# Feature-map attention and a maxout feed-forward on one core: numerators from 64-row matmul pairs, with the row maxima applied as a factor on GpSimd

## The chip, the cores and the metric

The kernel runs on one core of a Trainium2 chip. The metric is the device time of one execution in microseconds. Below, PE is TensorE, DVE is VectorE, ACT is ScalarE, POOL is GpSimd and SP is the engine that issues most DMAs.

## The reference

Attention without a softmax: q and k of each of 8 x 8 heads (576 tokens, 64 channels) are projected to 128 features and turned to two exponentials, and the output feeds a maxout layer. With the shapes cut to what matters:

```python
def phi(x):                                   # x: (8, 8, 576, 64)
    proj = np.einsum('bhsd,df->bhsf', x, w_phi)              # df = 128
    proj = proj - np.max(np.abs(proj), axis=-1, keepdims=True)
    return np.concatenate([np.exp(proj), np.exp(-proj)], axis=-1)
q_p, k_p = phi(q), phi(k)
kv = np.einsum('bhsf,bhsd->bhfd', k_p, v)
z = np.sum(k_p, axis=2)
num = np.einsum('bhsf,bhfd->bhsd', q_p, kv)
den = np.einsum('bhsf,bhf->bhs', q_p, z)[..., None] + 1e-06
x = num / den                                 # then to (4608, 512)
h = maximum(maximum(x @ w1, x @ w2), x @ w3)  # 4608 x 768
out = h @ w_out                               # 4608 x 512, float32
```

With m the largest absolute projection of a row, the two halves are exp(p - m) and exp(-p + m): m doesn't cancel between them, but a common factor of both halves does (but for the 1e-06).

## The kernel before

Attention goes by 16 **units** of four heads, two units to a batch; the feed-forward goes by nine **chunks** of 512 tokens, one to a batch and a last one (chunk 8) of the 64 tokens that each batch has over. The steps of a unit, with the names used below:

- **loads**: q, k and v come as 128 x 1152 tiles (18 tiles of tokens by 64 channels). From unit 4 on q and k come in float32 through SP's queue (line 474) and POOL casts them into `qk_bf` (480); units 1 to 3 use a converting DMA that POOL issues (463). In `qk_bf` of units from 4 on, the columns of a token tile hold 64 channels of q, then 64 of k.
- **T**: a transposing DMA (512) gives `qkT`, q's channels on partitions 0 to 63, k's on 64 to 127.
- **G**: projections in 64-row matmuls, one of q and one of k at a time (535), into `psq` and `psk`. ACT makes the exponentials `Ek` of k (548); DVE reduces the maxima of q into `mqp`, those of k into `mk` (554).
- **R, V**: PE transposes the maxima of q into `pmT` (562), `mT` is a copy of it (566), and a DMA writes it as one row into `qkT` (570), at partition 64, where a channel of k stood.
- **M**: `psm`, the features by tokens of q: one matmul of 512 columns for each four token tiles (614), whose weights `wphi_m` hold w_phi in 64 rows and -1 in the 65th, so that p - m comes out of the product, though the matmul takes all 128 rows. ACT makes the two `Eq` of it (627), with scales 1 and -1.
- **vab**: POOL multiplies v with a factor `em` from the maxima of k, one instruction for each sign (589).
- **K**: `kvps`, keys times values in 64-row matmuls (643), and their copy `kv_sb` (648).
- **N and x**: numerators and denominators `psn`, 20 matmuls of 65 columns in two steps for each pair of heads (661), and the division on DVE (667, 668).
- **X**: a transposing DMA (691) of `x_sb` into `xT`, by which the chunk of the unit's batch becomes ready.

A chunk multiplies xT with w2 - w1 and w3 - w1 (`ups`, 714; the differences are made once at the start, 784), takes the larger of both and zero on ACT (722) and DVE (724, 720), and makes the down product `ops`: from these maxima with w_out (746), and straight from xT with w1 times w_out (741), which is multiplied once at the start (812). It is copied out at 754 and stored at 761.

What sets the order: `manual_schedule()` leaves it to the program. `PLAN` is a table with one word for each step, number, engine, buffer slots and a start; `plan()` hands the steps their engine and slots from it and issues the code in the table's order. Every engine works its own queue in order. The eight PSUM banks are one pool of slots, `bank`, for all tiles in PSUM. `fill()` puts idle products (`idler`) into gaps of PE's table.

Of the kernel before, what the change touches and what calls it, by code (L numbers as in the profile page):

```python
# [12 lines left out]
ALU = mybir.AluOpType  # L13
# [37 lines left out]
QK = 3  # L51
OSB = 4
GATES = (None, (0, 0), (1, 0), (2, 0))
# [43 lines left out]
0G@0.70 2D0@0.70 4A@0.70 10S0@0.70 3D@0.90 6S0@1.18 1G@1.25 8S@1.66 86G0@1.75 13S@2.14 85G@2.60 15S0@2.62 1076G@3.45 12A1@3.98  # L97
158G2@4.25 7D@4.96 159G@5.10 5D@5.46 16T1@5.61 9A@5.94 1079G@5.95 17D0@6.30 22T002300@7.08 27T45@7.30 26D@7.55 30D@8.15 14A@8.43
25D@8.76 23A@9.05 20T6@9.20 18T7@9.31 31D@9.37 21D@9.97 227G1@10.01 28A@10.12 19D@10.20 42T14@10.35 29A@10.62 45D@10.81
32T26@10.96 24A@11.11 46D@11.15 37T75@11.26 35D@11.49 34A@11.60 89T1@11.60 91T3@12.04 47A0@12.09 40D@12.10 44A@12.34 48G0@12.48  # L100
39A@12.68 90D1@12.71 61T20@12.86 33A@13.16 64T7@13.31 92D@13.33 228G@13.60 38A@13.65 36D@13.95 95T111311@14.10 66A@14.14
49G@14.45 41D@14.56 65A@14.63 43A@15.12 99D@15.16 110T67@15.27 63A@15.46 50G@15.57 55T5@15.61 98D@15.77 1077G@15.85 111A@15.94
1090T4@16.06 113D@16.38 62A@16.43 1088T1@16.66 56A@16.91 114D@16.98 67T2@17.26 97A@17.40 1086T6@17.49 1089D0@17.59 51A@17.89
69A@18.14 87D1@18.21 53G@18.29 58T0@18.34 1087D@18.34 88S@18.46 68A@18.48 57A@18.82 164T1@18.89 361S1@18.94 1091D@18.96
59A@19.30 93T2@19.34 52G@19.41 162T6@19.45 165D2@19.59 112A@19.79 166T5@19.90 163D@20.21 60A@20.28 105T41@20.36 54G@20.52
1078G@20.80 106A@20.83 108D@20.83 70T070@20.95 96A@21.32 160D2@21.44 167D@21.54 161S@21.69 94D@21.76 109D@21.98 100T64@22.05
296S0@22.17 115T53@22.27 101A@22.52 72D@22.59 362S1@22.65 1094T2@22.75 119D@22.96 102A@23.02 117A@23.50 104D@23.66 116A@23.84
1096T0@24.05 107A@24.18 103D@24.26 124A1@24.68 118D@24.87 120A@24.93 127G1@25.07 71A@25.18 1095D@25.21 183T003400@25.44
1097A@25.59 173T16@25.66 168T57@25.88 123A@26.09 177D@26.13 1098T2@26.23 185A@26.24 170A@26.73 186D@26.74 125G@27.00 175A@27.22
176D@27.35 137T01@27.52 184A@27.71 171D@27.95 77T30@27.98 126G@28.12 138A@28.23 1092T1@28.29 78D0@28.56 139A@28.71 172D@29.18  # L110
1099A@29.20 122G@29.23 79T5@29.58 174A@29.70 187D@29.79 75T3@29.90 1093A@30.18 140T0@30.21 121G@30.35 229D3@30.39 131T2@30.44
76D1@30.50 141A@30.69 73T6@30.89 142A@31.03 80D0@31.11 128T4@31.21 132A@31.37 11G@31.47 364G0@31.62 74D1@31.73 178T13@31.76
133A@31.85 143T105@31.98 130A@32.34 181D@32.35 129A@32.82 182D@32.96 188T26@33.08 233T1@33.31 145A@33.33 192D@33.57 144A@33.73
134T4@33.88 191D@33.91 196A0@34.13 234D0@34.25 146T51@34.34 190A@34.38 198G0@34.53 148T0@34.65 135A@34.72 147D0@34.90
235T2@35.06 231T1@35.17 189A@35.20 149D1@35.52 199A@35.55 136A@35.70 152T5@35.74 193T6@36.05 232D@36.14 179A@36.18 81T0@36.29
83T4@36.60 197G@36.62 169A@36.67 153D0@36.76 150T1@36.91 194A0@37.16 154T7@37.31 236D@37.38 180A@37.41 195S@37.56 151D1@37.60
242T115611@37.72 84A@37.90 247T23@38.05 155D@38.22 297S0@38.34 156T1@38.39 82D@38.69 230S@38.82 215T047@38.87 157A@38.95
1080D@39.16 426S1@39.30 249A@39.60 1081D@39.78 1104T0@40.09 244A@40.09 1082D@40.40 248A@40.58 1106T1@40.95 250D@41.02 216A@41.07
365G@41.37 251D@41.63 1102T4@41.81 1107A1@42.06 246D@42.23 1105A@42.56 366S1@42.64 1110T2@42.67 245D@42.84 243A@43.06
1084D@43.45 1108T3@43.54 1103A@43.55 1111A@44.05 1085D@44.07 252T10@44.50 217A@44.55 1083D@44.69 257T56@44.72 237T42@44.83  # L120
1109A@44.95 1112T7@45.17 240D@45.31 259A@45.45 299G2@45.66 239A@45.79 255D@45.91 1124T3@46.04 254A@46.28 1113D@46.52 253A@46.77
# [119 lines left out]
1421S@265.97 1431A@266.06 1444T4@267.11 1416D2@267.36 1411T@267.97 1417S@268.12 1445D@268.22 1443D@268.84 1454T0@269.26  # L241
1412D0@269.51 1459T@270.12 1413S@270.28 1455T@271.41 1460D1@271.66 1461S@272.43 1462T2@272.70 1456A3@272.95 1463T@273.56
1457S@273.71 1474T7@274.85 1475T@275.07 1464D2@275.10 1466T1@275.39 1476A0@275.64 1467T@275.82 1465S@275.87 1477A@275.89
1470T4@276.47 1471T@276.68 1468A1@276.72 1469A@277.09 1472D3@277.25 1473S@277.68
"""


# [627 lines left out]
```

## Time and profile before

| | us |
|---|---|
| median of 3 runs | 285.63 |
| lowest and highest run | 283.97, 286.08 |
| span of the profiled execution | 282.5 |
| its own time around the span | not given; median less span is 3.1 |
| POOL casts of q and k (line 480), 24 | 27.5 |
| POOL products with v (line 589), 36 | 68.2 |
| DVE reductions (line 554), 160 | 97.3 |
| ACT exponentials of k and of q (548, 627), 320 | 160.0 |

In the profile a row of a group names the line, the engine, the operation, what it writes and reads, how often, its busy time and the mean duration in ns, and behind the second bar how long the engine stood idle just ahead of such instructions and what ended that. Durations of matmuls overlap, since they are pipelined: the distance from one start to the next is what one costs. Rows of the timeline begin with start and duration. PEld is the load of weights into PE, and SPq and POOLq are the engines' DMA queues.

### The profile page before, as it was taken

How to read it: one execution, taken by the hardware profiler on the slowest of the kernel's cores; microseconds unless marked ns; L12 is line 12 of the kernel's file. 1: busy time of each engine (PE TensorE's matmuls, PEld its weight loads, DVE VectorE, ACT ScalarE, POOL GpSimd, SP SyncE). 2: the span in 40 equal slices, each digit the busy share in tenths (PEclk: the TensorE clock that was granted, in tenths of full speed). 3: DMA queues.
4: the chain of work that ended last, by engine and by line, in shares of the span. 5: the costliest groups of instructions: out<-in, count | busy, mean ns of one | idle time of the engine just before them, and what ended most of it. 6: DMA issues, size and time to landing. Idle time of an engine off the chain costs nothing.

```text
span 282.5 us, 8556 instructions
## 1 busy us (share of the span) xinstructions
PE 271.2 (96%) x3521; PEld 154.0 (54%) x3560; DVE 211.6 (75%) x443; ACT 192.3 (68%) x449; POOL 113.2 (40%) x106
## 2 busy tenths in 40 slices
PE   8888979999999999999999999999999999999995
PEld 3565764566555644764556456555455465444443
DVE  4998989998877888679989876997477594254141
ACT  2897979898889779998585879977707961311111
POOL 8373567748176418913760563053033600000000
PEclk9999999999999999999999999999999999999999
DMA  7999999888999999999797866954975105600154
GB/s 202 240 206 282 280 273 240 266 204 167 300 363 198 175 308 300 194 165 277 212 199 129 246 235 124 166 102 167 186 177 116 40 4 104 137 2 0 37 123 139
DMA packets 68337, 51.45 MB, mean 182 GB/s; under 512 B 48778, under 2 KB 53066, under 8 KB 68298
## 3 DMA queue, kind: packets, MB, share of 16 engines
q1 hardware_dynamic: 63876, 45.74, 66.8%
q0 software_dynamic: 4000, 4.92, 10.0%
q8 instruction: 28, 0.46, 0.7%
q10 hardware_dynamic: 422, 0.24, 0.3%
q14 instruction: 11, 0.09, 0.1%
HBM read 34.64 MB, written 9.44 MB: 156 GB/s over the span
## 4 chain that ended last, share of the span: by engine, by line
PE 80%; DMA 11%; DVE 4%; issue 2%; SPq 1%; DVEq 0%
PE ups L714 31%; PE ops L746 14%; PE ops L741 10%; DMA wout_bf<-in_moe_w_out_dram 6%; PE psn L661 6%; PE kvps L643 5%; PE psm L614 5%; PE psq L535 4%; PE pm L812 2%; DMA out_dram<-osb 2%; DMA xT<-x_sb 2%; DVE x_sb L668 2%; DMA k_raw<-in_k_dram 1%; DVE mqp L554 1%; DVE mk L554 1%
## 5 line engine op out<-in xcount | busy, mean ns | idle before, releaser
L714 PE MATMUL ups<-xT,w_bf 128*128 128x512 bf16 x416 | 100.3, 379 | 1.4 <-DMA xT<-x_sb 0.3
L589 POOL TENSOR_TENSOR vab<-v_raw,em 128x1152 bf16<-128x1152 f32 (+1 forms) x36 | 68.2, 1907 | 67.2 <-ACT em L585 50.9
L548 ACT ACTIVATE Ek<-psk 128x512 bf16<-128x512 f32 (+1 forms) x160 | 80.8, 569 | 13.9 <-PE psk L535 10.1
L627 ACT ACTIVATE Eq<-psm 128x512 bf16<-128x512 f32 (+1 forms) x160 | 79.2, 570 | 7.3 <-PE psm L614 7.0
L714 PEld LDWEIGHTS <-w_bf 128*128 128x128 bf16 x432 | 41.0, 98 | 47.4 <-issue 0.4
L554 DVE TENSOR_REDUCE mqp<-psq 128x4 bf16<-128x512 f32 (+1 forms) x80 | 48.8, 631 | 6.3 <-PE psk L535 4.4
L746 PE MATMUL ops<-wout_bf,hT 128*128 128x512 bf16 (+2 forms) x215 | 49.3, 367 | 1.0 <-issue 0.5
L554 DVE TENSOR_REDUCE mk<-psk 128x4 f32<-128x512 f32 (+1 forms) x80 | 48.5, 628 | 2.4 <-PE psk L535 1.7
L720 DVE TENSOR_TENSOR hT<-hT,ups 128x512 bf16<-128x512 bf16 x54 | 36.1, 682 | 16.4 <-PE ups L714 12.7
L668 DVE TENSOR_TENSOR x_sb<-psn,rden 128x320 bf16<-128x320 f32 x64 | 31.5, 492 | 2.2
L746 PEld LDWEIGHTS <-hT 128*128 128x128 bf16 x228 | 21.1, 98 | 21.7
L722 ACT ACTIVATE hT<-ups 128x512 bf16<-128x512 f32 x33 | 19.1, 603 | 17.3 <-PE ups L714 15.8
L661 PEld LDWEIGHTS <-Eq 128*128 128x128 bf16 x640 | 25.0, 97 | 7.8 <-ACT Eq L627 0.2
L754 DVE COPY osb<-ops 128x512 f32<-128x512 f32 (+1 forms) x22 | 14.7, 669 | 16.8 <-PE ops L746 16.0
L661 PE MATMUL psn<-kv_sb,Eq 128*128 128x65 bf16 x640 | 26.9, 194 | 0.2 <-DVE mqp L554 0.2
L754 ACT COPY osb<-ops 128x512 f32<-128x512 f32 (+2 forms) x16 | 8.9, 562 | 23.2 <-PE ops L746 22.6
L741 PE MATMUL ops<-xT 128*128 128x512 bf16 x90 | 24.1, 380 | 0.3
L535 PE MATMUL psq<-w,qkT 64*128 64x128 bf16 x288 | 24.3, 217 | 0.1
L535 PE MATMUL psk<-w,qkT 64*128 64x128 bf16 x288 | 24.0, 217 | 0.4 <-ACT Eq L627 0.4
L535 PEld LDWEIGHTS <-qkT 64*128 64x128 bf16 x576 | 16.5, 94 | 12.0 <-issue 8.9
L614 PE MATMUL psm<-qkT,wphi_m 128*128 128x512 bf16 (+1 forms) x70 | 22.1, 358 | 0.0
L480 POOL CAST qk_bf<-q_raw 128x1152 bf16<-128x1152 f32 x12 | 13.8, 1147 | 20.3 <-DMA out_dram<-osb 9.4
(73 smaller groups left out, 230.9 us busy)
## 6 DMA issues: line engine op xcount, KB each, us to landing
v_raw<-in_v_dram SPq DMA_DIRECT2D x16, 576.0 KB
out_dram<-osb SPq DMA_DIRECT2D x64, 128.0 KB
q_raw<-in_q_dram SPq DMA_DIRECT2D x12, 576.0 KB
k_raw<-in_k_dram SPq DMA_DIRECT2D x12, 576.0 KB
w_bf<-in_moe_w_dram POOLq DMA_DIRECT2D x3, 768.0 KB, 20.3
qk_bf<-in_k_dram POOLq DMA_DIRECT2D x3, 288.0 KB, 13.9
qk_bf<-in_q_dram POOLq DMA_DIRECT2D x3, 288.0 KB, 13.4
wout_bf<-in_moe_w_out_dram POOLq DMA_DIRECT2D x1, 768.0 KB, 17.7
```

Of the source, the lines that this page charges most:

```text
L535: nc.tensor.matmul(ps()[:, i, :], lhsT=cols[r, :], rhs=w2[r, c, :], start=True, stop=True)
L548: nc.scalar.activation(Ek[s]()[:, tiles_of(t0, n), :], of(1), EXP, scale=1.0 - 2.0 * s)
L554: nc.vector.tensor_reduce((mq, mk)[c]()[:, tiles_of(t0, n)], of(c), AXX, ALU.max, apply_absolute_value=True)
L589: (nc.vector if n_.eng == "DVE" else nc.gpsimd).tensor_tensor(vab()[:, g, t0:t1, 0:D], vb()[:, t0:t1, :], em()[:, g, t0:t1].unsqueeze(2).t ...
L614: nc.tensor.matmul(psm()[:, 0:w], lhsT=wphi_m, rhs=rhs, start=True, stop=True)
L627: nc.scalar.activation(Eqb()[s][:, cols], psm()[:, 0:w], EXP, scale=1.0 - 2.0 * s)
L661: nc.tensor.matmul(psn()[:, c, :], lhsT=Eqb()[g][:, t0:t0 + P], rhs=kv()[:, pr, ab, g, :], start=(g == 0), stop=(g == 1))
L668: nc.vector.tensor_tensor(x_sb()[:, pr, :, ab, :], psn()[:, :, 0:D], rden().to_broadcast([P, 5, D]), ALU.mult)
L714: nc.tensor.matmul(ups(), lhsT=w_bf[i + 1][:, ct, j * P:(j + 1) * P], rhs=tokens_of(ct), start=(ct == 0), stop=(ct == CT - 1))
L720: nc.vector.tensor_tensor(hT()[:, j, :], hT()[:, j, :], ups(), ALU.max)
L741: nc.tensor.matmul(ops_()[:, 0:width], lhsT=tile_of(ct, tt), rhs=line_w[c_i > MOVE][:, ct, cols], start=(ct == 0), stop=False)
L746: nc.tensor.matmul(ops_()[:, 0:width], lhsT=hT()[:, j, tt * P:(tt + 1) * P], rhs=wout_bf[:, j, cols], start=False, stop=(j == JT - 1))
```

## The change

Units 0 to 3 stay as they are. From unit 4 on (`FROM`), a second function `attention_b` stands in for `attention`:

- q and k come by converting loads that POOL issues, into a `qk_bf` that holds all of q and then all of k; it has four slots instead of three. The float32 tiles of v, and of unit 0's q and k, share one pool of four slots (`RAW`).
- After T, partitions 0 to 63 hold one token tile and 64 to 127 the next, so that 64-row pairs are two token tiles of the same tensor. G does the tiles of q first, then those of k; the last tile of both is done as a full matmul of 256 columns against `w2`, which holds zeros beside w_phi.
- M no longer uses the row of maxima: two 64-row matmuls of 512 columns, for two banks of `psm`, go side by side. M needs only T, no longer R and V.
- The exponentials of q have constant offsets instead (`SHIFTS`): exp(p - 79) and exp(-p + 9). `Eq` has three slots instead of two.
- The maxima become a factor: `mT` is exp(-2m + 88), a DMA writes it to a row in memory (`row`), another broadcasts that row to 128 partitions (`fac`, one slot), and POOL multiplies the first half of `Eq` with it, in three instructions, two of 1024 elements and one of 256 for each partition. Numerators wait for these.
- The table `PLAN` is new as a whole, from the first step on.

```diff
-QK = 3
+QK = 4
+FROM = 4
+FAC = 1
+RAW = 4
+SHIFTS = (88.0, -79.0, 9.0)
...
-0G@0.70 2D0@0.70 4A@0.70 10S0@0.70 3D@0.90 6S0@1.18 1G@1.25 8S@1.66 86G0@1.75 13S@2.14 85G@2.60 15S0@2.62 1076G@3.45 12A1@3.98
...
-            raws[u] = [buf(f"{x}_raw", 4 if x == "v" else 2, [P, UT, D], FP32) for x in "qkv"]
+            raws[u] = [buf("raw", RAW, [P, UT, D], FP32) if x == "v" or u == 0 else None for x in "qkv"]
...
-    NE = 2
+    NE = 3
...
+    def attention_b(u):
...
+                def main(what=what):
+                    nc.gpsimd.dma_start(by_pairs(qk()[:, what]), rows_of(what, u, 0, 2))
+                cast[what, 0] = nd("L", {"POOL": 0.85}, main, [], [qk], pipe=FULL_BF, lat=2.1, packet=PACKET_BF)
...
+                def proj(c=c, t0=t0, pss=pss):
+                    for i in range(4):
+                        for h in range(2):
+                            r = slice(h * D, (h + 1) * D)
+                            nc.tensor.matmul(pss[h]()[:, i, :], lhsT=tiled(c)[r, t0 + i, :], rhs=w2[r, h, :], start=True, stop=True)
...
+                nc.tensor.matmul(pss[c](), lhsT=tiled(c)[:, NT - 1, :], rhs=w2, start=True, stop=True)
...
+        n_mt = nd("mT", {"ACT": 0.25}, lambda: nc.scalar.activation(mT(), pmT()[0:UT, :], EXP, bias=shift[0:UT, 0:1], scale=-2.0),
+                  [n_r, n_const], [pmT, mT], locks=[pmT])
+        row = scratch("row", 2, [1, 2, UT, D], BF16)
+        n_v = nd("V", {"ACT": 0.7, "SP": 0.7}, None, [n_mt], [mT, row], lat=2.2, pipe=0.1)
+        n_v.fn = lambda: queue_of[n_v.eng].dma_start(row()[0].rearrange("a t i -> t a i"), mT().rearrange("t (a i) -> t a i", i=D))
+        fac = buf("fac", FAC, [P, 2, UT, D], BF16)
+        n_f = nd("F", {"SP": 0.5, "ACT": 0.5}, None, [n_v], [row, fac], lat=2.0, pipe=1.4)
+        n_f.fn = lambda: queue_of[n_f.eng].dma_start(fac(), row().to_broadcast([P, 2, UT, D]))
...
+                    nc.scalar.activation(e_tiles(s)[:, ts], psm()[:, 0:n * P].rearrange("p (t a i) -> p t a i", a=2, i=D), EXP,
+                                         bias=shift[:, 1 + s:2 + s], scale=1.0 - 2.0 * s)
...
+                for h in range(2):
+                    r = slice(h * D, (h + 1) * D)
+                    nc.tensor.matmul(psms[h](), lhsT=w2[r, h, :], rhs=tiled(0)[r, t0:t0 + 4, :], start=True, stop=True)
+            a = nd("M", {"PE": 0.22}, mm, turned_by(0, t0, t0 + 4) + [n_phi], [qkT, Eqb] + psms, mode=1)
...
+                e = Eqb()[0][:, 0:UT * P].rearrange("p (a t i) -> p a (t i)", a=2, i=D)[:, :, t0 * D:t1 * D]
+                nc.gpsimd.tensor_tensor(e, e, fac()[:, :, t0:t1].rearrange("p a t i -> p a (t i)"), ALU.mult)
+            facs.append(nd("f", {"POOL": 0.12 + 0.205 * (t1 - t0)}, scale, [n_f] + [n_ for g_, n_ in eqs[0] if g_ == g], [fac, Eqb]))
...
+                a = nd("N", {"PE": 0.32}, nmm, [n_kvs[ab]] + facs[pr:pr + 2] + [n_ for g_, n_ in eqs[1] if pr <= g_ <= pr + 1], [Eqb, kv, psn, x_sb])
...
-        attention(u)
+        (attention if u < FROM else attention_b)(u)
```

Three places of the new order. First PE, at a step M. Before, a full matmul stood between numerators of unit 7 (`Eq_0` names a slot of `Eq`, `wphi_m` the weights with the row of -1):

```order
L661 LDWEIGHTS Eq_0_76
L661 MATMUL psn<-kv_sb,Eq_0_76 128x65
L614 LDWEIGHTS wphi_m
L614 MATMUL psm<-qkT,wphi_m 128x512
L661 LDWEIGHTS Eq_0_75
L661 MATMUL psn<-kv_sb,Eq_0_75 128x65
```

In the changed kernel a pair of M (lines 850) of unit 9 stands right ahead of a step of G (775) of unit 10, `w_75` being `w2`:

```order
L901 LDWEIGHTS Eq_1_81
L901 MATMUL psn<-kv_sb,Eq_1_81 128x65
L850 LDWEIGHTS w_75
L850 MATMUL psm<-qkT,w_75 128x512
L850 LDWEIGHTS w_75
L850 MATMUL psm<-qkT,w_75 128x512
L775 LDWEIGHTS qkT
L775 MATMUL psq<-w_75,qkT 128x128
```

So two matmuls stand for two of the four, next to other 64-row work.

Second PE, behind the last numerators of unit 7, which chunk 3 waits for. Before, the down products of chunk 2 (line 746) came next, and there were two more groups of them ahead of chunk 3's first up product:

```order
L661 LDWEIGHTS Eq_0_76
L661 MATMUL psn<-kv_sb,Eq_0_76 128x65
L746 LDWEIGHTS hT
L746 MATMUL ops<-wout_bf,hT 128x512
L746 LDWEIGHTS hT
L746 MATMUL ops<-wout_bf,hT 128x512
```

Now the last projections of unit 9 (line 786) come next, then numerators of unit 8 (`Eq_1`):

```order
L901 LDWEIGHTS Eq_2_83
L901 MATMUL psn<-kv_sb,Eq_2_83 128x65
L786 LDWEIGHTS qkT
L786 MATMUL psq<-w_75,qkT 128x256
L786 LDWEIGHTS qkT
L786 MATMUL psk<-w_75,qkT 128x256
L901 LDWEIGHTS Eq_1_80
L901 MATMUL psn<-kv_sb,Eq_1_80 128x65
```

All down products of chunk 2 now stand ahead of this place; from here to chunk 3's first up product there are only steps of attention.

Third POOL, in the middle of the program. Before, casts of q and k stood between the products with v:

```order
L480 CAST qk_bf<-k_raw 128x18x64
L589 TENSOR_TENSOR vab<-v_raw,em 128x18x64 x2
L480 CAST qk_bf<-q_raw 128x18x64
L599 CAST vab<-em 128x36
L819 COPY w_bf<-xT 128x2x512
L480 CAST qk_bf<-k_raw 128x18x64
```

Now loads are issued there, and the scalings of `Eq` with `fac` stand between the products:

```order
L729 DMA qk_bf<-in_q_dram 128x2x576
L821 TENSOR_TENSOR vab<-raw,em 128x18x64 x2
L867 TENSOR_TENSOR Eq_1_80<-Eq_1_80,fac 128x2x512
L867 TENSOR_TENSOR Eq_1_80<-Eq_1_80,fac 128x2x128
L867 TENSOR_TENSOR Eq_1_80<-Eq_1_80,fac 128x2x512
L829 CAST vab<-em 128x36
```

The casts are gone, and each scaling is ahead of products with v of other units in the queue.

More of the change, by code (lines that the diff above doesn't have):

```diff
@@ L101 @@
[L101 to L109, printed above, removed]
@@ L240 @@
[L240 to L244 removed]
+0G@0.72 10S0@0.73 2D0@0.85 3D@1.07 6S1@1.19 1G@1.29 4A@1.30 8S@1.65 1076G@1.79 13S@2.11 15S2@2.57 86G0@2.59 85G@3.44 12D1@3.63
@@ L323, in fixed, with scratch @@
         return Buf(pool, lambda b: tiles[b.index])
+    dram = ctx.enter_context(tc.tile_pool(name="dram", bufs=1, space=bass.MemoryType.DRAM))
+    def scratch(name, n, shape, dtype):
+        pool = slots.setdefault(name, Slots(n))
+        return Buf(pool, lambda b: dram.tile(shape, dtype, name=name, tag=f"{name}{b.index}"))
     def bank(name, shape, dtype=FP32):
@@ L397, in zeros @@
         nc.vector.memset(wphi_m, 0.0)
+        for i, c in enumerate(SHIFTS):
+            nc.vector.memset(shift[:, i:i + 1], c)
         nc.vector.memset(wphi_m[D:D + 1, :], -1.0)
```

429 lines of the change are left out of this document (295 added, 134 removed).

## The prediction

> **What bounds the kernel now.** I read the busy shares first, then the stretches of time with their mean rates, then the chain that ended last, then the groups of instructions.
>
> ```profile
> PE 271.2 (96%) x3521; PEld 154.0 (54%) x3560; DVE 211.6 (75%) x443; ACT 192.3 (68%) x449; POOL 113.2 (40%) x106
> 0.00:20.00 20.00, 17.51 (x229) 10.45 (x229) 15.61 (x38) 13.46 (x30) 12.09 (x21) 1.00 1.03 216
> 20.00:40.00 20.00, 17.46 (x416) 12.84 (x412) 17.14 (x43) 17.19 (x45) 11.72 (x12) 1.00 1.12 271
> 120.00:140.00 20.00, 19.54 (x260) 10.85 (x258) 17.60 (x37) 16.09 (x37) 7.97 (x7) 1.00 1.03 226
> 220.00:240.00 20.00, 19.89 (x228) 11.17 (x229) 12.85 (x30) 11.63 (x28) 5.25 (x6) 1.00 0.21 41
> PE 80%; DMA 11%; DVE 4%; issue 2%; SPq 1%; DVEq 0%
> ```
>
> The stretches' columns are busy time of PE, its weight load, DVE, ACT and POOL, then clock, DMA share and GB/s. PE loses 5.0 us in the first 40 us, where DMA is full. After that it stands still for 0.1 to 0.5 us in every 20, at full clock, and it carries 80% of the chain. So a column that PE need not stream counts in full, and so does each place where PE has nothing to do. POOL, at 40%, has room.
>
> **The columns that go.** Twelve units change, 4 to 15. The prices are distances between starts on PE in the timeline.
>
> ```profile
> 178.01 0.38 PE L614 MATMUL psm<-qkT,wphi_m 128*128 128x512 bf16 x1
> 178.22 0.47 PE L661 MATMUL psn<-kv_sb,Eq 128*128 128x65 bf16 x10
> 174.11 0.27 PE L614 MATMUL psm<-qkT,wphi_m 128*128 128x256 bf16 x1
> 174.22 1.03 PE L714 MATMUL ups<-xT,w_bf 128*128 128x512 bf16 x4
> 162.53 1.03 PE L714 MATMUL ups<-xT,w_bf 128*128 128x512 bf16 x4
> 163.49 0.23 PE L535 MATMUL psq<-w,qkT 64*128 64x128 bf16 x1
> 163.49 0.23 PE L535 MATMUL psk<-w,qkT 64*128 64x128 bf16 x1
> 163.55 0.22 PE L535 MATMUL psq<-w,qkT 64*128 64x128 bf16 x1
> 176.67 0.22 PE L535 MATMUL psk<-w,qkT 64*128 64x128 bf16 x1
> 176.82 1.04 PE L741 MATMUL ops<-xT 128*128 128x512 bf16 x3
> ```
>
> A 512-column matmul takes 0.215 us, a 256-column one 0.11. Two 64-row matmuls start together, a pair of 128 columns every 0.055. In M four 512-column matmuls per unit become two pairs: 12 x 2 x 0.215 = 5.2 us less. The last one, 256 columns, becomes two of 128: nothing. The last step of G was two pairs (0.11) and becomes two 256-column matmuls (0.22): 12 x 0.11 = 1.3 more. Going into 64-row work costs 0.10 (four ups from 162.53 end at 163.39, G starts at 163.49), and so does leaving it (the pair at 176.67 ends at 176.72, the next starts at 176.82). The order has 43 runs of 64-row matmuls where there were 42, since M's pairs mostly stand beside G or K: 0.2 more. Sum: 5.2 - 1.3 - 0.2 = 3.7 us less for PE.
>
> The Trainium skill (TensorEngine Tiling (Array Packing), Key Properties) says that a change of the tiling mode drains the engine; the trace agrees with its 0.10 us. If each of the 24 pairs stood alone, this would come to 24 x 0.2 = 4.8 us and leave nothing of the gain, which speaks against 64-row work in small pieces; by the order it doesn't happen here.
>
> **The hand-over to each chunk.** This is where I expect the gain to go. A chunk's first up products need xT, which a transposing DMA writes after the last division of its two units. Before chunk 3:
>
> ```profile
> 125.90 1.11 PE L661 MATMUL psn<-kv_sb,Eq 128*128 128x65 bf16 x30
> 127.80 4.66 DMA xT<-x_sb
> 132.50 1.67 PE ups L714 x7
> 124.60 0.57 SPq L474 DMA_DIRECT2D k_raw<-in_k_dram  x1
> 125.23 0.46 SPq L474 DMA_DIRECT2D q_raw<-in_q_dram  x1
> 131.60 1.15 POOL L480 CAST qk_bf<-q_raw 128x1152 bf16<-128x1152 f32 x1 [7.91 <-DMA q_raw<-in_q_dram]
> 236.09 1.33 SPq L691 DMA_TRANSPOSE xT<-x_sb  x1
> 239.58 0.75 POOL L831 COPY x_last<-xT 128x256 bf16<-128x256 bf16 x2 [13.54 <-DMA xT<-x_sb]
> ```
>
> Thirty numerator matmuls end at 126.85 (0.031 each), ups starts at 132.50: 5.65 us, 4.66 of them the DMA. The DMA's other bound is 3.49, from 236.09 until POOL could copy, late in the run. The 4.66 had two loads of 576 KB just ahead of it on its queue. Those loads leave SP's queue, so I take the middle, 4.1, and a hand-over of 5.1.
>
> PE's order says what covers it. Before chunk 3 there stood three groups of down products (4 + 6 + 6 matmuls of 0.215) and some G: PE waited 0.3 us. Now there is no down product left: two pairs and two 256-column matmuls, 20 numerator matmuls, five G pieces of 0.22, a transpose and two runs of 64-row work, in all 2.6 us. So PE waits 2.5, that is 2.2 more. At chunk 2 one group of down products stands less, and four numerator steps in a row make DVE finish 0.75 us later: 5.85 against 4.7 us of work, 1.15 more. At chunk 1: 5.1 against 4.8, 0.3 more. Chunks 4 to 7 keep 5.5 us or more of cover. Sum 3.65; with 3.49 for the DMA it is 2.1, with 4.66 it is 5.25.
>
> **POOL, the loads and the factor.** Prices per form:
>
> ```profile
> L589 POOL TENSOR_TENSOR vab<-v_raw,em 128x1152 bf16<-128x1152 f32 x28 | 59.1, 2124 | 62.6 <-ACT em L585 47.8 <-DMA v_raw<-in_v_dram 12.3 <-issue 2.5
> L589 POOL TENSOR_TENSOR vab<-v_raw,em 128x576 bf16<-128x576 f32 x8 | 9.1, 1149 | 4.6 <-ACT em L585 3.1 <-DMA v_raw<-in_v_dram 1.5
> L819 POOL COPY w_bf<-xT 128x1024 bf16<-128x1024 bf16 x2 | 2.1, 1042 | 0.0
> L480 POOL CAST qk_bf<-k_raw 128x1152 bf16<-128x1152 f32 x12 | 13.7, 1148 | 13.8 <-DMA k_raw<-in_k_dram 13.8
> L463 POOL DMA_DIRECT2D qk_bf<-in_k_dram x3 | 2.5, 817 | 0.0
> L463 POOL DMA_DIRECT2D qk_bf<-in_q_dram x3 | 2.2, 719 | 4.1 <-issue 4.1
> L784 DVE TENSOR_TENSOR w_bf<-w_bf 128x1024 bf16<-128x1024 bf16 x6 | 3.8, 680 | 0.0
> L566 ACT COPY mT<-pmT 18x128 bf16<-18x128 bf16 x12 | 3.0, 248 | 11.1 <-PE pmT L562 10.1 <-ACT kv_sb L648 1.0
> L570 SPq DMA_DIRECT2D qkT<-mT x12: 767/799/924, 37.8 to 222.2; - x12
> q1 hardware_dynamic: 63876, 45.74, 66.8%
> q0 software_dynamic: 4000, 4.92, 10.0%
> ```
>
> The two L589 forms give 0.17 us and 1.69 ns an element. A scaling of 1024 elements is then 1.9 us, of 256 0.6; the copy of 1024 bounds it below at 1.04. I take 1.9, the same operation. POOL loses 24 casts (27.5 us) and gains 24 load issues of 0.77 (18), 36 scalings (12 x 4.4 = 53) and five subtractions of w that DVE did in 0.68 (9.5): 113 + 53 = 166 us, 59%. It isn't the bound, but it works in order, and each scaling stands ahead of a later unit's vab. DMA: 24 loads leave q1 (14.2 MB), 24 of half the bytes join q0, and 12 broadcasts of 7.1 MB in all are new; q1 has 66.8% of the span for 45.74 MB, q0 10.0% for 4.92, so -20.7 + 14.4 + 10.3 = 4% of the span more, which 77% can take.
>
> The Trainium skill (GPSIMD Engine Reference, section 3.1) gives 4497 ns for a two-input operation on 2048 elements and prefers VectorE for it. By that, 2.2 ns an element, a scaling would take 2.25 us as an estimate and the forecast would be some 1 us later; the rows here have 1.69.
>
> The factor's path replaces the row's: the transpose pmT (0.22), an exponential instead of the copy (0.25), a DMA of 4.5 KB to memory (issue 0.80), a broadcast DMA back of 576 KB (issue 0.5), two scalings (3.8), numerators: 5.6 us plus two landings. The first landing is at most 2.9: unit 13 now has 4.2 us of PE work between transpose and M, and no matmul of L614 waited. The second is bounded by loads of that size: 6.4 us for the q load above (125.23 to 131.60, two together), and for one alone
>
> ```profile
> 67.97 0.57 SPq L474 DMA_DIRECT2D k_raw<-in_k_dram  x1
> 72.17 1.15 POOL L480 CAST qk_bf<-k_raw 128x1152 bf16<-128x1152 f32 x1 [2.33 <-DMA k_raw<-in_k_dram]
> ```
>
> 4.2 us. Landings together: up to 9.3, at best perhaps 6; I take 7.2, nearest to one load alone, so a path of 12.8. The new order gives PE, between pmT and the first numerators, 11.7 us of work in unit 11, 12.6 in unit 8, 12.9 in 9, 14.0 in 15 and 14.5 in 4, and more elsewhere. Late: 1.1 + 0.2, say 1.2 us; with 9.3 it would be 3.2 + 2.3 + 2.0 + 0.9 + 0.4 = 8.8, with 6 nothing. SP, too, is in order: the factor's DMA waits there for the row's, and stores and transposes behind it wait along; that is inside this bound.
>
> **The start.** The first weight is now issued ahead of unit 1's q and k, and all weights and unit 5's loads follow at once. That moves waits about more than it adds any; POOL's five subtractions (9.5 us against 3.4) stand ahead of up products of chunk 0. I price it at 0.3, between -1.5 (a third of the 5.0 us idle) and +1.5. DVE and ACT lose and gain under 5 us each, hidden by their 25% and 32% idle.
>
> **Sum.** -3.7 + 3.65 + 1.2 + 0.3 = 1.45: 284.0 us of span. The median of the three runs, 285.6, lies 3.1 above the span of the profiled execution, whose own time isn't given; so 287.1 us.
>
> **Rivals.**
> - The waits are absorbed: the hand-overs cost between nothing and 2.1, the factor is never late, the start gains up to 1.5. 282.5 - 3.7 is 278.8 us, with the 2.1 it is 280.9, so with the 3.1 between 280.4 and 284, about 282.3. For it: 24 loads leave the queue that the transposes use. Against: three hand-overs lose their cover by order, whatever the DMA does.
> - The factor is late (the other side). Place: POOL's scalings behind the broadcast, PE at the first numerators of units 11, 8, 9, 15, 4. It decides slower once the landings pass about 7.8 us together (2.9 of wait instead of 1.2); at 9.3 the time is 287.1 + 7.6 = 294.7. For it: loads of that size took 4.2 to 6.4. Against: the order leaves 12 us or more.
> - The pairs of M don't overlap, so the change doesn't do what it says: the 5.2 us stay, 292.3. Against: L535's pairs start together.
>
> **How the numbers follow.** Forecast 0.47, absorbed 0.20, factor late 0.27, pairs 0.06. The range, 281.5 to 292, takes in nearly all of the absorbed case and of the factor case what is up to 6 us late, and leaves out about 0.2; the forecast alone would be 285.3 to 289. A measurement tells about 1% from no change, here below 282.8 or above 288.5. Faster is some two thirds of the absorbed case, 0.13; slower is the factor, the pairs and the forecast's upper end, 0.35; the same 0.52.
>
> **What would show it.** M's 512-column matmuls as 64-row pairs starting together, and fewer PE columns; PE idle of 2 us or more ahead of chunk 3's first ups, put down to xT; POOL about 166 us with scalings of 1.9; numerators that wait for POOL in units 11 and 8 alone. The forecast is wrong if ups of chunks 1 to 3 don't wait, if numerators wait for the factor in most units, or if PE's idle in the first 40 us moves by over 1.5 us.

## The result, and the profile after

The changed kernel takes 315.07 us (median of 314.21, 315.94, 310.03 and 316.16) against 285.69 us for the kernel before, measured beside it: 1.094 times as long, with a 95% interval of 1.085 to 1.104. The forecast was 287.1 with a range of 281.5 to 292, so it is far out, on the slow side. Times in this text are medians of all runs of a kernel, while the ratios leave disturbed runs out; so differences between kernels are taken from the ratios, in points of 1%, which is 2.85 us.

The page of the changed kernel: busy time of each engine, the granted clock and the DMA engines' share in 40 slices of 7.8 us, and the two large queues (packets, MB, share of the 16 engines).

```profile
PE 280.4 (90%) x3514; PEld 155.0 (50%) x3550; DVE 209.4 (67%) x441; ACT 206.4 (66%) x454; POOL 168.7 (54%) x140
PEclk9999999998999979999999879999999999999999
DMA  7999996999889995899699989459766931440044
q1 hardware_dynamic: 58923, 38.14, 54.4%
q0 software_dynamic: 10528, 12.00, 25.0%
```

The span went from 282.5 to 312.4 us, 29.9 more. PE's idle time (span less busy) went from 11.3 to 32.0: 20.8 of it. PE's busy time grew by the other 9.2, although it has fewer columns to stream. POOL came out at 168.7 us, near the forecast's 166. What PE waited for, in us in total, times and the longest:

```profile
PE ups L938 <- DMA xT<-x_sb: 10.0, 4, 5.5
PE psn L901 <- POOL Eq L867: 6.7, 8, 1.8
PE psk L775 <- DMA qkT<-qk_bf: 3.8, 1, 3.8
```

So 13.8 us are waits for transposed tiles and 6.7 for scaled numerators. The stretches of the timeline (PE, its weight load, DVE, ACT, POOL, clock, DMA share, GB/s) show where; the three with most loss:

```profile
100.00:120.00 20.00, 12.63 (x176) 6.74 (x175) 11.61 (x26) 10.83 (x26) 12.14 (x9) 0.91 0.98 201
160.00:180.00 20.00, 15.47 (x285) 9.47 (x287) 14.75 (x31) 12.00 (x29) 12.08 (x11) 0.94 1.26 175
180.00:200.00 20.00, 17.67 (x159) 7.89 (x160) 9.96 (x18) 13.52 (x32) 13.33 (x8) 0.89 0.88 189
```

The losses stand in a few places, and there the clock is below 1.00; in the kernel before it was 1.00 in every such stretch until PE's work ended. PE's timeline at an earlier, shorter one (start, length, what):

```profile
74.97 0.75 PE L938 MATMUL ups<-xT,w_bf 128*128 128x512 bf16 x2 [2.16 <-DMA xT<-x_sb]
75.94 4.98 PE L938 MATMUL ups<-xT,w_bf 128*128 128x512 bf16 x16
```

The same columns as in the stretches above, for some 3.4 us at the end of each of the four longest waits for transposed tiles:

```profile
75.40:78.80 3.40, 3.40 (x10) 1.37 (x9) 1.95 (x4) 2.59 (x5) 0.00 (x0) 0.52 1.14 275
112.90:116.30 3.40, 2.90 (x7) 1.18 (x9) 0.00 (x0) 1.19 (x4) 1.11 (x1) 0.51 0.76 182
177.80:181.20 3.40, 3.18 (x11) 1.27 (x11) 2.92 (x5) 3.40 (x10) 0.79 (x1) 0.52 1.56 123
184.60:188.00 3.40, 3.40 (x11) 0.86 (x10) 1.29 (x2) 2.18 (x5) 0.71 (x2) 0.51 0.51 98
```

PE waits 2.16 us, and for some 3.4 us from then on it runs at half its clock: 16 matmuls take 4.98 us instead of 16 x 0.215 = 3.4. Four such stretches cost up to 4 x 1.7 = 6.8 us, most of the 9.2. A wait costs more than its length.

The chain that ended last names the two kinds of lateness (start, length, what):

```profile
171.27 13.02 DMA xT<-x_sb
184.30 0.04 issue
184.34 0.88 PE ups L938 x2
...
200.72 4.86 POOL Eq L867 x3
205.58 0.02 issue
205.60 4.27 DMA fac<-row
...
210.62 4.22 POOL Eq L867 x2
214.84 0.05 issue
214.89 0.24 PE psn L901 x2
```

A transposing DMA that was priced at 4.1 us took 13.02. And a broadcast of the factor left at 205.60, 0.02 us after the scalings of the unit before had ended: it had to wait for the one factor buffer. In the waits of SP's queue, where the broadcasts are issued (line 803), this stands five times:

```profile
SPq L803 <- POOL Eq L867: 12.8, 5, 3.1
```

### The profile page after: what moved, and what is told of

It reads as the page before. It is cut to its first block, busy times and chain, and to the rows that moved or that the text cites. A ratio compares the mean times of both kernels' runs of the same rounds, so it can differ in the third digit from the quotient of the medians.

```text
span 312.4 us, 8573 instructions
## 1 busy us (share of the span) xinstructions
PE 280.4 (90%) x3514; PEld 155.0 (50%) x3550; DVE 209.4 (67%) x441; ACT 206.4 (66%) x454; POOL 168.7 (54%) x140
## 2 busy tenths in 40 slices
DMA packets 70282, 51.46 MB, mean 165 GB/s; under 512 B 49186, under 2 KB 59618, under 8 KB 70242
## 3 DMA queue, kind: packets, MB, share of 16 engines
q1 hardware_dynamic: 58923, 38.14, 54.4%
## 4 chain that ended last, share of the span: by engine, by line
PE 29%; POOL 9%; DMA 9%; ACT 4%; issue 2%; DVE 1%; POOLq 0%
PE ups L938 13%; PE ops L970 8%; POOL Eq L867 7%; DMA xT<-x_sb 6%; PE ops L965 4%; DMA fac<-row 3%; ACT Eq L840 2%; PE psn L901 1%; POOL vab L821 1%; ACT Ek L764 1%; PE psm L850 1%; DVE x_sb L908 0%; PE psq L775 0%; PE kvps L883 0%; POOL qk_bf L729 0%
## 5 line engine op out<-in xcount | busy, mean ns | idle before, releaser
L867 POOL TENSOR_TENSOR Eq<-Eq,fac 128x1024 bf16<-128x1024 bf16 (+1 forms) x36 | 58.3, 1639 | 41.5 <-ACT Eq L840 21.3
L840 ACT ACTIVATE Eq<-psm,shift 128x512 bf16<-128x512 f32 (+1 forms) x120 | 69.1, 671 | 12.1 <-PE psm L850 8.9
L821 POOL TENSOR_TENSOR vab<-raw,em 128x1152 bf16<-128x1152 f32 x24 | 50.6, 2121 | 37.7 <-ACT em L817 19.1
L758 DVE TENSOR_REDUCE mqp<-psq 128x4 bf16<-128x512 f32 (+1 forms) x60 | 36.3, 631 | 7.4 <-PE psq L775 7.2
L758 DVE TENSOR_REDUCE mk<-psk 128x4 f32<-128x512 f32 (+1 forms) x60 | 36.6, 628 | 3.9 <-PE psk L786 2.5
L948 DVE TENSOR_SCALAR hT<-ups 128x512 bf16<-128x512 f32 x23 | 15.8, 688 | 24.9 <-PE ups L938 24.9
L901 PEld LDWEIGHTS <-Eq 128*128 128x128 bf16 x480 | 18.7, 98 | 13.7 <-POOL Eq L867 9.3
L908 DVE TENSOR_TENSOR x_sb<-psn,rden 128x320 bf16<-128x320 f32 x48 | 23.6, 492 | 1.7
L641 ACT ACTIVATE Eq<-psm 128x512 bf16<-128x512 f32 (+1 forms) x40 | 20.8, 570 | 1.5 <-PE psm L628 0.7
L603 POOL TENSOR_TENSOR vab<-raw,em 128x576 bf16<-128x576 f32 (+1 forms) x12 | 17.5, 1471 | 6.1 <-ACT Ek L562 2.9
## 6 DMA issues: line engine op xcount, KB each, us to landing
qk_bf<-in_k_dram POOLq DMA_DIRECT2D x15, 288.0 KB, 11.5
```

Source lines behind the costliest of these rows:

```text
L758: nc.vector.tensor_reduce((mq, mk)[c]()[:, ts], of(), AXX, ALU.max, apply_absolute_value=True)
L821: nc.gpsimd.tensor_tensor(vab()[:, g, t0:t1, 0:D], vb()[:, t0:t1, :], em()[:, g, t0:t1].unsqueeze(2).to_broadcast([P, t1 - t0, D]), ALU.mult)
L840: nc.scalar.activation(e_tiles(s)[:, ts], psm()[:, 0:n * P].rearrange("p (t a i) -> p t a i", a=2, i=D), EXP, bias=shift[:, 1 + s:2 + s], ...
L867: nc.gpsimd.tensor_tensor(e, e, fac()[:, :, t0:t1].rearrange("p a t i -> p a (t i)"), ALU.mult)
L901: nc.tensor.matmul(psn()[:, c, :], lhsT=Eqb()[g][:, t0:t0 + P], rhs=kv()[:, pr, ab, g, :], start=(g == 0), stop=(g == 1))
L908: nc.vector.tensor_tensor(x_sb()[:, pr, :, ab, :], psn()[:, :, 0:D], rden().to_broadcast([P, 5, D]), ALU.mult)
```

## The experiments

Two theories stood against each other, and a third that blames neither. A: the converting loads meet the transposing DMAs on the DMA engines. B: POOL's scalings and the factor's DMAs make the numerators late. C: the new order leaves PE without cover whatever the transfers do. The changed kernel and the first seven runs make up every combination of the three added costs. The loads' edit also frees the transposing DMAs of q and k from waiting for a load, since they read a finished tile instead. The three edits are:

```diff
 loads' bytes out (units 4 to 15)
-nc.gpsimd.dma_start(by_pairs(qk()[:, what]), rows_of(what, u, 0, 2))
+nc.gpsimd.dma_start(qk()[:, what, 0], rows_of(what, u, 0, 2)[:, 0, 0:D])
-in_=qk().rearrange("p c t d -> p (c t d)"))
+in_=wout_bf.rearrange("p j n -> p (j n)")[:, 0:2 * UT * D])
 most of the scaling out
-nc.gpsimd.tensor_tensor(e, e, fac()[:, :, t0:t1].rearrange("p a t i -> p a (t i)"), ALU.mult)
+nc.gpsimd.tensor_tensor(e[:, :, 0:D], e[:, :, 0:D], fac()[:, :, t0], ALU.mult)
 factor's DMAs out (the scalings read a tile of ones)
-n_v.fn = lambda: queue_of[n_v.eng].dma_start(row()[0].rearrange("a t i -> t a i"), mT().rearrange("t (a i) -> t a i", i=D))
-n_f.fn = lambda: queue_of[n_f.eng].dma_start(fac(), row().to_broadcast([P, 2, UT, D]))
+n_v.fn = lambda: None
+n_f.fn = lambda: None
```

> Leaves out nearly all bytes of the converting loads: units 4 to 15 load one tile of 18 of q and of k, and their transposes read a finished weight tile (the output of these units is that of other inputs). Theory A, the converting loads collide with the transposing DMAs: the four long waits for transposed tiles (2.2 + 5.5 + 3.8 + 2.1 = 13.6 us in the profile after) and about 4 us of low clock behind them go, so about 297 us (293 to 301). Theory B, POOL's scalings and the factor's path make the kernel late, and the transposes only follow: at most 5 us less, 310 or more. Theory C, the order itself leaves the hand-overs without cover: 309 to 315, with waits for xT ahead of chunks 1 and 2 of 2 us or more.

> Leaves out most of the scaling on POOL: each of the 36 multiplies 128 elements instead of 1024 or 256, some 65 us of POOL less; the factor is still computed, sent and waited for. Theory B: the waits for scaled numerators (6.7 us of PE) go, and most of the later lateness with them: 303 us or less. Theory A: waits for xT and qkT stay at 10 us or more, 307 to 312. Theory C: 309 to 315.

> Leaves out the factor's two DMAs (12 rows to memory, 12 broadcasts back, 7.1 MB); the scalings multiply by ones, for the same time on POOL, and wait for no landing. If the landings of the factor set the scalings' time (three waits of POOL, 10.1 us in all): 303 to 308. If POOL's own work in order sets it: 311 to 315. Theory A: the traffic counts a little, 308 to 312, with the long waits for transposed tiles still there.

> All three left out at once: the bytes of the converting loads, most of the scaling, and the factor's DMAs. What is left is the new order with its pairs of 64 rows. Theories A and B together: 278 to 284 us, no wait for xT over 1 us. Theory C, the order itself: 292 or more, with PE waiting for xT ahead of chunks 1 to 3. The prediction's hand-over term (3.65 us) would make it 282 to 286.

> Leaves out the bytes of the converting loads and the factor's DMAs; the full scalings stay (by ones). With nothing of the three the kernel takes 287.8 us, with all of them 315.1. If POOL's 65 us of scaling cost time by themselves: 292 to 298, with numerators waiting for POOL. If they cost only when a landing ahead of them is late: 288 to 290, and numerators wait less than 2 us in all.

> Leaves out the bytes of the converting loads and most of the scaling; the factor's DMAs stay and are waited for. If the broadcasts slow the transposing DMAs on their own (median landing of xT 4.9 us with them and without the loads, 3.4 without both): 291 to 296, with landings of xT near 4.9 and of qkT near 6.7. If they matter only together with POOL's scalings: 288 to 290.

> Leaves out most of the scaling and the factor's DMAs; the converting loads stay whole. If the loads collide with the transposing DMAs whatever POOL does: 292 to 296, with one or more waits for xT over 2 us and low clock behind them. If loads and factor need each other to be late: 288 to 290.

| left in the kernel | us, median | ratio to before (95%) |
|---|---|---|
| nothing of the three (order alone) | 287.8 | 1.014 (1.008 to 1.019) |
| scaling | 290.3 | 1.013 (1.008 to 1.018) |
| broadcast | 290.4 | 1.018 (1.007 to 1.028) |
| loads | 297.9 | 1.044 (1.037 to 1.051) |
| scaling, broadcast (run without loads' bytes) | 298.1 | 1.037 (1.028 to 1.046) |
| loads, scaling (run without broadcast) | 295.2 | 1.026 (1.020 to 1.032) |
| loads, broadcast (run with small scaling) | 303.7 | 1.055 (1.046 to 1.064) |
| all three (the changed kernel) | 315.1 | 1.094 (1.085 to 1.104) |

Theory C falls as the main cause: the order alone is 1.4% slower, not 9. Neither A nor B alone is enough. The loads alone add 3.0 points (8.5 us). Scaling or broadcast alone adds nothing that can be told; together they add 2.3 (6.5 us). The remaining 2.7 points come when all three are there. Loads with scaling came out 1.8 points below loads alone, with intervals that don't touch, so a share is good to some two points; that moving one thing also moves where the transfers meet is the likely reason, but isn't shown.

Of the expectations, theory A's range was met without the loads' bytes (298.1), and the second case with the scaling alone (290.3) and, at its edge, with the broadcast alone (290.4). The rest missed: small scalings (303.7) just past B's bound, no broadcast (295.2) below every case, the order alone (287.8) between its two cases, and the loads alone (297.9) above A's range, with the waits that A named.

The landing times of the transposing DMA of the normalized numerators (least, median, most), with the order alone:

```profile
DMA to landing us min/median/max: 2.9/3.4/5.6
```

and with the loads added:

```profile
DMA to landing us min/median/max: 2.9/4.5/9.3
```

What PE waited for, in the same two kernels, first the order alone:

```profile
PE ups L940 <- DMA xT<-x_sb: 2.5, 2, 1.9
```

then with the loads (for qkT no wait is listed in either):

```profile
PE ups L940 <- DMA xT<-x_sb: 10.3, 4, 6.7
```

In the changed kernel the landings are 3.3/5.7/13.0. Where only loads are left, the worst place has three loads on POOL and then the transpose on SP's queue, which already takes 4.21 us to be issued:

```profile
98.44 0.76 POOL L731 DMA_DIRECT2D qk_bf<-in_q_dram  x1
99.20 0.72 POOL L731 DMA_DIRECT2D qk_bf<-in_k_dram  x1
99.92 0.72 POOL L731 DMA_DIRECT2D qk_bf<-in_q_dram  x1
100.87 4.21 SPq L917 DMA_TRANSPOSE xT<-x_sb  x1
110.24 0.61 PE L940 MATMUL ups<-xT,w_bf 128*128 128x512 bf16 x1 [6.67 <-DMA xT<-x_sb]
```

The Trainium skill (DMA: Bandwidth & Descriptors, section SWDGE vs HWDGE vs iDMA) says that software and hardware queues feed the same engines, which serve them in turn. These rows agree: a load on a queue of its own is not out of the transposes' way.

**The pairs by themselves.** The order alone, with M's pairs undone:

```diff
-nc.tensor.matmul(psms[h](), lhsT=w2[r, h, :], rhs=tiled(0)[r, t0:t0 + 4, :], start=True, stop=True)
+nc.tensor.matmul(psms[h](), lhsT=w2[:, h, :], rhs=tiled(0)[:, t0:t0 + 4, :], start=True, stop=True)
```

> As the kernel with all three left out, and the pairs of 64 rows in M undone: the four 512-column matmuls of a unit run over 128 rows again (the other 64 rows of the weights are zeros), so 24 x 0.215 = 5.2 us more on PE, less up to 1 us for changes of the tile's rows. If the prediction's price of the pairs holds: 287.8 + 4.2 to 5.2 = 292 to 293. If PE has room there because it waits for DVE and ACT: 288 to 290.

289.6 us, ratio 1.017 (1.010 to 1.024), against 287.8 and 1.014 with the pairs. The two profiled spans are 289.9 and 285.6; the first holds one stretch of 3.4 us at a clock of 0.52, some 1.7 us, so 2.6 us are left for the pairs. The 289.6 lie in the second expectation's range (288 to 290). The runs put the pairs at some 1 to 3 us; the two intervals overlap, so they may bring nothing, but not the 4.2 or more of the first expectation.

**Do the loads cost by where they meet?** Two kernels with the loads whole and the factor's work out, the loads at other places of POOL's order; in the second, some wait on POOL for the landing of a transpose (a one-element copy from its tile). The new places are numbers in the plan; the first lines are from the first kernel, the last two from the second:

```diff
+if n.kind == "L" and 68.5 < n.start < 73.0:
+    n.start += 5.0
+elif n.kind == "L" and 98.5 < n.start < 101.0:
+    n.start = 108.2 + n.start / 1000
...
+if u in (8, 13):
+    nc.gpsimd.tensor_copy(gated, xT[0:1, 1, 2, 0:1] if u == 8 else units[10]["qkT"]()[0:1, 0, 0:1])
```

> As the kernel in which only the converting loads are left (most of the scaling and the factor's DMAs are left out; 297.9 us), with the same loads at other places of POOL's order, away from the transposing DMAs of the numerators: those issued beside the transposes ahead of chunks 1 and 2 some 5 and 9 us later, three loads of units 14 and 15 later, the last one of unit 12 earlier. Nothing is loaded less. If the loads cost by colliding with these transposes: 290 to 293, no wait for xT over 2.5 us (6.7 before). If they cost by landing late themselves, or by their bytes wherever they stand: 296 or more, and new waits for qkT.

> As the kernel in which only the converting loads are left (most of the scaling and the factor's DMAs are left out; 297.9 us), with the loads kept apart from the transposing DMAs that the up products wait for: eight loads wait on POOL for the transpose of unit 3's result, two for the transpose of unit 10's q and k, the others stand at places without such a transpose. If a meeting with these transposes is all that the loads cost: 289 to 292, no wait for xT over 2.5 us, median landing of xT back near 3.5. If they cost by their bytes in any place: 296 or more.

298.3 us (ratio 1.041, 1.032 to 1.049) and 300.6 (1.056, 1.050 to 1.063): both lie in the second range (296 or more), and neither is faster than the 297.9 they started from. The traces show where the time went. In the first, the place that had cost 6.67 us is mended: the transpose is issued in 1.45 us and PE waits 1.88, as with no loads at all. But three loads now meet a later transpose:

```profile
101.87 1.45 SPq L926 DMA_TRANSPOSE xT<-x_sb  x1
106.56 0.82 PE L949 MATMUL ups<-xT,w_bf 128*128 128x512 bf16 x2 [1.88 <-DMA xT<-x_sb]
161.81 0.76 POOL L740 DMA_DIRECT2D qk_bf<-in_q_dram  x1
161.96 1.48 SPq L926 DMA_TRANSPOSE xT<-x_sb  x1
162.57 1.43 POOL L740 DMA_DIRECT2D qk_bf<-in_k_dram  x2
170.34 1.01 PE L949 MATMUL ups<-xT,w_bf 128*128 128x512 bf16 x2 [3.06 <-DMA xT<-x_sb]
```

In the second, no landing of xT takes more than 5.3 us (9.3 before), but loads at 131.96 to 134.87 meet a transpose of q and k, whose issue takes 6.96 us, and two transposes of xT stand behind it on SP's queue:

```profile
137.12 6.96 SPq L753 DMA_TRANSPOSE qkT<-qk_bf  x1
144.18 3.72 SPq L927 DMA_TRANSPOSE xT<-x_sb  x2
148.73 1.86 PE L950 MATMUL ups<-xT,w_bf 128*128 128x512 bf16 x4 [5.89 <-DMA xT<-x_sb]
```

So the meeting shows place by place, but these two arrangements only moved it. Whether a third is free of it, or the loads cost as much in any place, these runs can't tell.

The first kernel's places in the whole kernel, alone and with the scalings on DVE:

```diff
-nc.gpsimd.tensor_tensor(e, e, fac()[:, :, t0:t1].rearrange("p a t i -> p a (t i)"), ALU.mult)
+nc.vector.tensor_tensor(e, e, fac()[:, :, t0:t1].rearrange("p a t i -> p a (t i)"), ALU.mult)
```

> The changed kernel whole, with the converting loads at those other places alone. If the collision costs as much here as where the loads are the only one of the three left: 303 to 309 instead of 315. If the factor's path sets the end here anyway: 312 or more.

> As the kernel with moved loads, and the 36 scalings on DVE instead of POOL. DVE took 0.68 us for a subtraction of this size where POOL takes 2.13 for the scaling. If it is the time of the scaling that makes the factor's path late (4.8 us a unit on POOL, some 1.6 on DVE): 3 to 8 us below the kernel with moved loads, at best near 292. If it is the landing of the broadcast that makes it late: no better, or slower, since DVE's evacuations stand behind the wait.

312.1 us (ratio 1.092, 1.082 to 1.102) and 310.3 (1.078, 1.070 to 1.087). Moving the loads does not help here either. On DVE the large scaling takes a third of POOL's 2.12 us, and by the ratios 1.4 points (4 us) are won, with intervals that overlap: the lower end of what was expected if the scaling's time counts, and far from 292. The group of large scalings on DVE, by form (busy us, mean ns, idle before them):

```profile
L876 DVE TENSOR_TENSOR Eq<-Eq,fac 128x1024 bf16<-128x1024 bf16 x24 | 17.6, 733 | 15.8 <-DMA fac<-row 15.8
```

In the waits of the same execution, which was the longest of its four (315.7 us; the shortest took 306.8), DVE's for the factor and PE's for DVE:

```profile
DVE Eq L876 <- DMA fac<-row: 16.5, 4, 11.7
PE psm L859 <- DVE x_sb L917: 10.9, 1, 10.9
```

Here DVE stands 11.7 us for one factor, and PE stands behind DVE. Whether the shorter executions had this wait isn't shown.

**One factor buffer?** Without the loads' bytes, scaling and broadcast cost 2.3 points together and next to nothing alone. The factor now lies in two tiles (token columns 0 to 7 and 8 to 17), each with its own broadcast, so that one half can leave while the other is still in use:

```diff
-fac = buf("fac", FAC, [P, 2, UT, D], BF16)
+fac = buf("fac", FAC, [P, 2, 8, D], BF16)
+fac2 = Buf(slots.setdefault("fac2", Slots(1)), lambda b: work.tile([P, 2, UT - 8, D], BF16, name="fac2", tag="fac2"))
...
-n_f.fn = lambda: queue_of[n_f.eng].dma_start(fac(), row().to_broadcast([P, 2, UT, D]))
+queue_of[n_f.eng].dma_start(fac(), row()[:, :, 0:8].to_broadcast([P, 2, 8, D]))
+queue_of[n_f.eng].dma_start(fac2(), row()[:, :, 8:UT].to_broadcast([P, 2, UT - 8, D]))
...
```

> As the kernel without the bytes of the converting loads (298.1 us), with the factor in two tiles of 8 and 10 columns of tokens, each with a broadcast of its own; bytes, scalings and order stay. If the one buffer is what makes scaling and broadcast late together: the next unit's first half leaves after the first of the three scalings, so units in a row stand some 6 to 7 us apart instead of 9, and the time falls to 290 to 294. If the broadcast's bytes or POOL's time make it late: 296 or more.

> The changed kernel whole, with the loads kept apart and the factor in two tiles; nothing is left out. If the two causes are those: 292 to 300 instead of 315. It can't come below the order alone, 287.8, so it stays slower than the kernel before. If other causes weigh more: 305 or more.

297.0 us (ratio 1.044, 1.039 to 1.050) against 298.1 (1.037, 1.028 to 1.046): nothing is won. With the loads kept apart, in the whole kernel: 312.3 (1.100, 1.096 to 1.105), a miss by 12 us. The trace of the first showed a fault of the experiment: units 10 and 11 free columns 8 to 17 first, while columns 0 to 7 were sent first. Turned round:

```diff
+loads = [(fac(), row()[:, :, 0:8], 8), (fac2(), row()[:, :, 8:UT], UT - 8)]
+for dst, src, n in loads[::-1] if u in (6, 9, 11, 12) else loads:
+    queue_of[n_f.eng].dma_start(dst, src.to_broadcast([P, 2, n, D]))
...
+if n.kind == "f" and n.u == 7 and n.start > 127.0:
+    n.start = 124.7
```

> As the kernel with the factor in two tiles (small converting loads, 297.0 us), but units 6, 9, 11 and 12 send first the half that the unit before frees first, and unit 7 scales its first 8 columns first. Nothing else changes. If the one buffer makes scaling and broadcast late together: the scalings of units 10 and 11, 9.7 us apart with the halves, stand 8 us apart or less, PE waits for POOL in all under 4 us (6.1 before), and the time falls to 289 to 294. If POOL's own work in order (two products of v of 2.1 us and three scalings, 9 us a unit) sets the distance: 295 to 299, and the waits stay.

290.2 us, ratio 1.020 (1.016 to 1.024), as the first expectation said: 2.4 points (7 us) less than with the halves in one order, and 1.6 (5 us) less than with one buffer, for the same bytes and the same scalings. What differs is which half four units send first, and the place of one scaling of unit 7. POOL's scalings of units 10 and 11 in its timeline, with one buffer (without the loads' bytes):

```profile
186.01 4.84 POOL L867 TENSOR_TENSOR Eq<-Eq,fac 128x256 bf16<-128x256 bf16 x3
195.47 4.83 POOL L867 TENSOR_TENSOR Eq<-Eq,fac 128x256 bf16<-128x256 bf16 x3 [4.63 <-DMA fac<-row]
```

and with the halves turned:

```profile
180.36 4.83 POOL L875 TENSOR_TENSOR Eq<-Eq,fac 128x256 bf16<-128x256 bf16 x3 [0.44 <-DMA fac<-row]
186.43 0.67 POOL L875 TENSOR_TENSOR Eq<-Eq,fac 128x256 bf16<-128x256 bf16 x1 [1.24 <-DMA fac<-row]
```

They stood 9.46 us apart, one pass of scalings (4.84) and one landing (4.6) in a row (9.72 with the halves in one order), and now 6.07. PE's wait for scaled numerators, 6.6 us in the kernel without the loads' bytes, 6.1 with the first halves, became:

```profile
PE psn L909 <- POOL Eq L875: 2.5, 3, 1.5
```

The same halves in the whole kernel, nothing left out:

> The changed kernel whole, nothing left out, with the factor in two tiles of which the one free first is sent first. If the factor buffer and the loads are two causes that add: 298 to 303 us (297.9 with the loads alone, 2.4 for what the halves leave), instead of 315, with waits for transposed tiles of 8 us or more and for POOL under 4. If the loads make the factor late in any case: 306 or more.

305.1 us, ratio 1.066 (1.058 to 1.075), 2.8 points (8 us) below the changed kernel, between the two expected ranges. Of the waits one came as expected and one didn't. Those for transposed tiles are 8.3 us (7.6 for xT and 0.7 for qkT), where the changed kernel had 13.8. Those for POOL were to fall under 4 us, and stayed where they were (6.7 before):

```profile
PE psn L909 <- POOL Eq L875: 6.4, 4, 4.1
138.68 4.81 POOL L875 TENSOR_TENSOR Eq<-Eq,fac 128x1024 bf16<-128x1024 bf16 x3 [4.46 <-DMA fac<-row]
```

The longest of them is at unit 7. Its two broadcasts were issued by 131.68, and the next scaling began at 138.68, 7 us later, where the landings in the changed kernel had been 4.1 to 4.9. So with the loads there the factor lands late too, as the second expectation supposed, and the 8 us can't be put down to shorter waits for POOL. This is the execution of 309.3 us, the longest of the four.

What the loads cost beside the halves is 4.6 points (13 us), more than the 8.5 us that they cost alone. This is the best whole version found. It doesn't beat the kernel before, and the order without any of the three costs, at 287.8, doesn't either.

## Why the prediction was wrong

- **The step that failed first: DMA as a sum of bytes.** The prediction put the transfers at "4% of the span more, which 77% can take" and so at nothing. The bytes are right (51.46 MB against 51.45), but not their time: 54.4 + 25.0% of 312.4 us are 248 us, against 66.8 + 10.0% of 282.5, which are 217. That is 11% of the old span more, not 4. And what PE waits for is the landing of one transpose, which went from 3.4 us (median, order alone) to 5.7, and to 13.0 at worst. The loads cost 8.5 us alone and 13 beside the turned halves.
- **The hand-over.** Taken with 4.1 us for the transpose, bounds 3.49 to 4.66. Without the three costs the landing is 3.4, and PE waits 1.9 us for xT ahead of chunk 2, where 1.15 was priced. Ahead of chunk 3, which had most of the term (2.2), no wait for xT is listed, against the sign that the prediction named. The time was lost there all the same, 5.0 us from unit 7's last numerators to the first up product (5.1 were forecast, with 2.6 of work in it), but in gaps of 0.2 to 0.4 us, for DVE and ACT; the transpose, issued at 134.01, would land at 137.4 with the median of 3.4, so the two limits lie close together. The order alone:

```profile
132.12 0.79 PE L903 MATMUL psn<-kv_sb,Eq 128*128 128x65 bf16 x20
135.59 0.38 PE L777 MATMUL psq<-w,qkT 64*128 64x128 bf16 x7 [0.37 <-DVE mqp L760]
137.74 6.54 PE L940 MATMUL ups<-xT,w_bf 128*128 128x512 bf16 x28 [0.20 <-DVE mqp L760]
```

  And "Chunks 4 to 7 keep 5.5 us or more of cover" holds only for such landings: the 13.02 us transpose stands ahead of chunk 4. The term of 3.65 was mis-sized with its main input, the landing; waits for xT and for qkT came to 13.8. Its upper bound adds up to 5.3, not 5.25, which changes nothing.
- **The factor.** The chance was 0.27 and the time up to 294.7, with landings over 7.8 us as the point from which it decides. Landings did not decide. Those of the broadcast were 4.1 to 4.9 us, inside the assumption; the first one, of the row, did pass its bound of 2.9 (SP stood for it seven times, up to 6.1 us), but not in the units where PE waited. The missing link was the single buffer, FAC = 1, for which the prediction has no term: a broadcast can't leave until the last scaling of the unit before has ended. So the wait falls on units that come close behind another: 4, 7, 11 and 15, with 1.1 to 2.4 us of PE each. Of these 4, 11 and 15 were named, for another reason. The prediction priced each unit's path from its own transpose on, and never asked what the path waits for at its other end. The turned halves show it without the loads' bytes: 5 to 7 us, and waits of PE for POOL of 2.5 us instead of 6.1 or 6.6. In the whole kernel they bring 8 us, but there these waits stay at 6.4, so by which path they do stays open.
- **The columns.** M's pairs do start together, as the distance to the next instruction on PE shows (0.23 us for two 512-column matmuls, then G):

```profile
119.10 0.39 PE L850 MATMUL psm<-qkT,w 64*128 64x512 bf16 x2
119.33 0.39 PE L775 MATMUL psq<-w,qkT 64*128 64x128 bf16 x8
```

  So the rival that they don't is out. But the pairs brought 1 to 3 us instead of 5.2, or less. With the order alone the span is 285.6 us at full clock, where the kernel before had 282.5; with the forecast's 3.7 less to stream that is some 7 us in which PE does not stream. From 100 to 140 us PE is idle for 3.4 us, where it was 0.8 before: the wait ahead of chunk 2 and the gaps ahead of chunk 3. Where the rest goes stays open. (Busy times don't tell: the profile before lacks 39 matmuls of 3560 by its weight loads, that of the order alone none.)
- **POOL and the scaling.** 168.7 us against 166. The large scaling took 2.12 us against 1.9, and with the scaling alone left in the ratio is that of the order alone, so this mis-sizing cost nothing by itself. The start came out within its bounds: chunk 0's first weights are loaded at 42.28 us against 41.78. The 3.1 us between span and time were 1.8 in the profiled execution (314.21 against 312.4).
- **The clock.** No term for it: up to 6.8 us, behind waits that the terms above should have held.

For columns, hand-over and start the forecast was +0.25 us; the order alone measured +1.4%, 4 us. For the factor it was 1.2, for the transfers nothing; the two came to 8.0 points, some 23 us.

## What to carry to other kernels

When loads move to another queue, ask which latency-bound transfer they now meet, not how many per cent of the DMA engines are free; the price is the landing time of that transfer where PE waits for it. For every buffer that a new path passes through, count the copies: with one, a transfer and the work on it run in a row, and units close together wait for their sum. Where one stall is found, look at the granted clock behind it before the rest of the loss is put down to something else.

## What the runs showed of the hardware

- Around waits of PE the granted clock fell to half for 3.4 us, or for 6.8 and 10.2 us at waits of 6.67 and 5.89 us (loads alone; loads kept apart). These two longer stretches began inside the wait, and 3.8 and 5.9 us of them lay behind it. It is not a matter of length alone. In the changed kernel waits of 2.16 and 2.12 us did it and one of 1.84 did not. With the order alone a wait of 1.9 us passed at full clock; with the pairs undone the same wait was followed by 3.4 us at 0.52. With the halves turned 1.53 us was enough; with the loads moved in the whole kernel, waits of 3.02 and 2.96 us passed at full clock. The Trainium skill (TensorE: Matmul & The Clock Gate, section Why this matters for your kernels) warns of idle gaps over about 3 us; here half of that was enough once, and 3.02 us was not.
- A scaling of 128 x 1024 elements in bf16 took 2.12 us on POOL and 0.73 on DVE.
- The converting loads of 288 KB landed 7.7 us (q, median) and 11.5 us (k) after their issue on POOL, the broadcast of 576 KB on SP's queue 4.3 us after its own.
